# An attention and MLP kernel with a written-out order: the order and the PSUM banks are replaced, and the keep-busy products at the end are regrouped

## The chip, the cores and the metric

The kernel runs on one NeuronCore of a Trainium2 chip. A core has five instruction streams that run side by side: TensorE (PE, matrix products into PSUM), ScalarE (ACT), VectorE (DVE), GpSimd (POOL) and SyncE (SP), which here only issues transfers. Each runs its own list strictly in order, and the lists wait for each other through semaphores. PSUM has eight banks of 128 x 512 float32; TensorE writes a bank, ScalarE or VectorE reads it, and only then may TensorE write it again.

The metric is the device time of one execution in microseconds. Three runs of the kernel before took 799.29, 800.50 and 801.38 us (median 800.5).

## The reference

Sequence 2048, width 640, 32 heads of 20, everything in bfloat16.

```
x  = A_x                                  # (1, 2048, 640)
xn = layernorm(x)
qkv = xn @ wqkv                           # 640 x 1920; 32 heads of 20
p  = softmax(q @ k.T * 20**-0.5)          # 32 matrices of 2048 x 2048
s  = concat(p @ v) @ wo                   # attention branch
h  = gelu(layernorm(xn) @ w1)             # MLP branch
hs = concat(h, its four quarters shifted by +1, -1, +2, -2 rows) @ w2
x1 = xn + hs
b  = x1 + gelu(layernorm(x1) @ w3) @ w4
return x + s * silu(b)
```

Most of the work is the softmax: 32 x 2048 x 2048 exponentials.

## The kernel before

The program first writes itself down as a list of 6,035 tasks (`Planner.task`): each has an engine, what it reads and writes, a function that emits its one to 16 instructions, and, for a product, the kind of PSUM bank it takes (`acq`) and which task gives the bank back (`rel`). Costs and due times in the list (`dur`, `due`, `DUE`) play no part in what is emitted. The order is not computed: the string `TABLE` spells it out. `Planner.follow` (line 218) reads two characters for a task's number and one more for each bank choice, and appends the task to its engine's list. So the string fixes the order of each of the five engines and the bank of each product, and nothing else; `plan_sync` (line 322) then puts in the semaphore waits that the data and the banks require, and `emit` writes the instructions.

One thing in the instructions does depend on the order. A pair of score products (`score_pair`, line 1587 and 1600) can be written in two ways: as two products that use 32 of the 128 rows of TensorE's array each (called the row form here, line 1587), or as eight products that use 32 of its columns each and the zero-padded copies `QM` of the queries (the column form, line 1600). `follow` sets the row form where the task stands behind a row-form task or just ahead of one or of another score pair, else the column form:

```
if t.flex and (pe_mode or (nx is not None and (nx.mode or nx.flex))):
    t.mode, t.dur = 1, self.row_dur
```

The last block of queries is worked in two halves (`last_half`, line 1407 on), where the same choice is between lines 1458 (row form) and 1462 (column form), with 256 columns instead of 512.

The work is staged so. At the start x is loaded, normalised on VectorE, ScalarE and POOL, transposed through TensorE (line 1066, copied out at lines 1074 and 1077) and projected to keys and queries of the first four heads (`prep`) and to values (`v_proj`). The attention then goes through eight quads of four heads, and in each through four blocks of 512 queries (`attn_quad`). For each of 16 key tiles two score pairs are computed. Most pairs go to ScalarE's exponential (line 1647, 128 x 1024 at a time); the rest go to VectorE, which makes an approximate exponential by arithmetic on the bit patterns (line 1671 from PSUM, then lines 1565 on POOL and 1567 on VectorE). The products with the values (lines 1380 and 1579) add up in bank 7. `normalise` turns, scales and stores a block's result: on POOL (`onT`, line 1707), then by SP's transfers `on` (turned) and `o` (to memory).

In between run the projections of later heads (`stack`, five times), which go to memory and come back by SP's transfers `fKT`, `fQT` and `fa` (`fetch`); from these a transfer `qm` makes the copies `QM` of each block's queries, which its score pairs need. The MLP branch runs in the gaps of TensorE as well: `b_w1`, `b_w2`, `b_w3`, `b_w4`, nearly all of their products from line 719. Its Gelu runs on ScalarE in six long operations (`gelu1`, line 1962, and `gelu3`, line 2054), each behind the VectorE copies `gt` (line 2047) of all its inputs. In the last quad the output projection and the output's last steps are mixed in (`part_qc`, `finish_qc`: `woa`, `wob`, `cmb`, `st_out`).

At two places TensorE computes products that nobody reads, to stay busy: 41 at the start (`warm`, line 892), and near the end those of `keep_busy` (lines 1402 and 1407), whose number and form are listed in `FLN`: pairs of a form (1 is two products in the row form, 0 four in the column form) and a count.

## Time and profile before

| | |
|---|---|
| runs | 799.29, 800.50, 801.38 us |
| the profiled execution | 798.07 us, of which 796.3 us from first to last instruction |
| first exponential of the attention starts | 30.66 us |
| last exponential starts | 787.83 us |
| last product on TensorE starts | 791.35 us |
| granted TensorE clock, mean | 0.999 |

The table has times of one profiled execution; it was 2.4 us faster than the median of the three runs. Busy times in the profile are sums of instructions, and on one engine instructions overlap a little: an exponential is shown with 1041 ns although the next can start after 904 ns. So a busy share near 97% does not yet mean that an engine never waits. The column "idle before, releaser" of a group, and the view of waits, say how long an engine stood still ahead of such instructions and whose signal ended it.

By stretches of the span, as the windows view gives them, ScalarE was busy 41.80 us of the first 50, 97.36, 96.33, 98.31, 99.83, 99.01 and 99.97 us of the six hundreds from 100 to 700, 48.64 of 700 to 750 and 35.00 of the 46 us that are left.

### The profile page before, as it was taken

How to read it: one execution, taken by the hardware profiler on the slowest of the kernel's cores; microseconds unless marked ns; L12 is line 12 of the kernel's file. 1: busy time of each engine (PE TensorE's matmuls, PEld its weight loads, DVE VectorE, ACT ScalarE, POOL GpSimd, SP SyncE). 2: the span in 40 equal slices, each digit the busy share in tenths (PEclk: the TensorE clock that was granted, in tenths of full speed). 3: DMA queues.
4: the chain of work that ended last, by engine and by line, in shares of the span. 5: the costliest groups of instructions: out<-in, count | busy, mean ns of one | idle time of the engine just before them, and what ended most of it. 6: DMA issues, size and time to landing. Idle time of an engine off the chain costs nothing.

```text
span 796.3 us, 29914 instructions
## 1 busy us (share of the span) xinstructions
PE 776.1 (97%) x13408; PEld 323.0 (41%) x13408; DVE 733.0 (92%) x1206; ACT 766.3 (96%) x802; POOL 353.1 (44%) x208
## 2 busy tenths in 40 slices
PE   8999999999999999999999999999999999999996
PEld 4443333334444333333434444334333343445454
DVE  8879899989999999999999999999988989999967
ACT  7899999999999999999999999999999999999994
POOL 5535234251546737663532443544233243352453
PEclk9999999999999999999999999999999999999999
DMA  5022373342121323434233231325224113133432
GB/s 167 3 73 60 72 173 77 84 102 57 35 53 29 76 43 84 86 70 93 57 83 61 40 96 41 69 56 93 53 51 112 26 20 86 20 96 85 135 90 85
DMA packets 138671, 57.58 MB, mean 72 GB/s; under 512 B 111040, under 2 KB 133744, under 8 KB 138544
## 3 DMA queue, kind: packets, MB, share of 16 engines
q1 hardware_dynamic: 138544, 55.68, 30.4%
q8 instruction: 105, 1.72, 0.9%
q14 instruction: 22, 0.18, 0.1%
HBM read 34.70 MB, written 10.33 MB: 57 GB/s over the span
## 4 chain that ended last, share of the span: by engine, by line
PE 49%; ACT 35%; DVE 11%; DMA 2%; issue 1%; POOL 1%; SPq 0%; DVEq 0%; POOLq 0%
ACT arena L1647 30%; PE psum L719 18%; PE psum L1587 12%; PE psum L1579 8%; PE psum L1380 6%; DVE arena L1671 5%; PE psum L1600 5%; DMA out_dram<-arena 2%; DVE arena L1567 1%; ACT arena L2054 1%; ACT arena L1962 1%; ACT arena L1629 1%; DMA arena<-in_A_x_dram 1%; POOL arena L1870 1%; PE psum L1066 1%
## 5 line engine op out<-in xcount | busy, mean ns | idle before, releaser
L1647 ACT ACTIVATE arena<-psum 128x1024 bf16<-128x1024 f32 x726 | 676.4, 1041 | 15.7 <-PE psum L1587 8.9
L1671 DVE TENSOR_SCALAR arena<-psum 128x512 uint16<-128x512 f32 x536 | 342.0, 682 | 24.5 <-PE psum L1587 20.7
L1565 POOL TENSOR_TENSOR arena<-arena 128x2048 int32<-128x2048 int32 x68 | 244.5, 3598 | 252.6 <-DVE arena L1567 172.7
L719 PE MATMUL psum<-arena 128*32 128x320 bf16 (+1 forms) x5776 | 323.1, 332 | 2.3 <-DVE arena L1567 1.0
L1587 PE MATMUL psum<-arena 32*128 32x512 bf16 x1660 | 203.0, 384 | 8.0 <-ACT arena L1647 3.5
L719 PEld LDWEIGHTS psum<-arena 128*32 128x32 bf16 x5776 | 142.6, 96 | 116.5 <-issue 23.2
L1579 PE MATMUL psum<-arena 128*22 128x512 bf16 x2144 | 185.6, 381 | 0.0
L1567 DVE TENSOR_SCALAR arena<-arena 128x4096 uint16<-128x4096 uint16 (+1 forms) x151 | 164.2, 1105 | 2.0 <-PE psum L1579 0.8
L1380 PE MATMUL psum<-arena 128*22 128x512 bf16 x1448 | 138.7, 382 | 0.1
L1587 PEld LDWEIGHTS psum<-arena 32*128 32x128 bf16 x1660 | 56.7, 91 | 179.1 <-ACT arena L1647 96.9
L1600 PE MATMUL psum<-arena 128*32 128x512 bf16 x1296 | 98.5, 380 | 0.5 <-ACT arena L1647 0.2
L1579 PEld LDWEIGHTS psum<-arena 128*22 128x22 bf16 x2144 | 50.0, 91 | 64.4 <-issue 33.2
L1707 POOL TENSOR_TENSOR arena<-arena 128x512 bf16<-128x512 f32 x30 | 40.8, 1359 | 73.1 <-DVE arena L1567 40.2
L1380 PEld LDWEIGHTS psum<-arena 128*22 128x22 bf16 x1448 | 35.8, 90 | 50.8 <-issue 25.8
L1600 PEld LDWEIGHTS psum<-arena 128*32 128x32 bf16 x1296 | 27.1, 95 | 34.6 <-ACT arena L1647 28.0
L2047 DVE CAST arena<-psum 128x512 bf16<-128x512 f32 x48 | 32.9, 686 | 3.9 <-PE psum L719 3.2
L1256 DVE CAST arena<-psum 128x512 bf16<-128x512 f32 x40 | 26.7, 684 | 1.2 <-PE psum L719 0.7
L929 DVE BATCH_NORM_STATS2 arena<-arena 128x6 f32<-128x320 bf16 x54 | 24.3, 481 | 1.2 <-DMA arena<-in_A_x_dram 1.2
L1699 DVE STREAM_TRANSPOSE arena<-psum 128x512 f32<-128x512 f32 x31 | 22.0, 711 | 3.3 <-PE psum L1380 2.2
L1629 ACT ACTIVATE arena<-psum 128x2048 bf16<-128x2048 f32 x13 | 24.7, 1903 | 0.0
L1870 POOL TENSOR_TENSOR arena<-arena 128x640 bf16<-128x640 bf16 x12 | 16.7, 1397 | 15.6 <-DMA out_dram<-arena 6.2
L946 POOL TENSOR_SCALAR arena<-arena 128x640 bf16<-128x640 bf16 x16 | 14.0, 876 | 18.5 <-DVE arena L1567 9.4
(125 smaller groups left out, 364.8 us busy)
## 6 DMA issues: line engine op xcount, KB each, us to landing
arena<-in_B_w_dram SPq DMA_DIRECT2D x48, 160.0 KB, 2.7
arena<-arena SPq DMA_DIRECT2D x124, 32.0 KB, 1.9
arena<-in_B_w_dram SPq DMA_DIRECT2D x4, 960.0 KB, 5.6
arena<-in_A_x_dram SPq DMA_DIRECT2D x8, 320.0 KB, 5.7
arena<-in_A_x_dram SPq DMA_DIRECT2D x16, 160.0 KB, 2.3
out_dram<-arena SPq DMA_DIRECT2D x16, 160.0 KB, 2.4
heads<-arena SPq DMA_DIRECT2D x120, 20.0 KB, 2.1
arena<-queries SPq DMA_DIRECT2D x28, 80.0 KB
```

The costliest lines, as they stand in the source:

```text
L719: ins = e.matmul(pb[32 * c:32 * c + 32, 0:N], lhsT(k, c), rhs(k, c), start=(k == 0), stop=(stop and k == nk - 1), tile_position=(0, 32 * c))
L1380: ins = e.matmul(pb[32 * i:32 * i + 22, 0:512], VA[:, ql, kts[i // 2], i, :], PT[:, slots[i // 2][0].slot, 512 * (i % 2):512 * (i % 2) + 512],
L1565: return e.tensor_tensor(dst.bitcast(I32), U[:, ub, 0:w].bitcast(I32), bass.AP(c.tensor, c.offset, [list(c.ap[0]), [0, w // 2]]), op=ALU.add)
L1567: fa if onp else lambda e, v=v, dst=dst: e.tensor_scalar(dst, U[:, ub, 0:w], EXP_B[v], None, op0=ALU.add),
L1579: ins = e.matmul(pb[32 * i:32 * i + 22, 0:512], wv, dst[:, at:at + 512].bitcast(BF16), start=first, stop=final, tile_position=(0, 32 * i))
L1587: return e.matmul(out, self.KT[32 * i:32 * i + 32, b, 128 * kt:128 * kt + 128], self.QT[32 * i:32 * i + 32, b, 512 * qc:512 * qc + 512], s ...
L1600: ins = e.matmul(out[32 * c:32 * c + 32, :], self.KT[:, b, 128 * kt + 32 * c:128 * kt + 32 * c + 32], self.QM[:, gb, 2 * a + jj, :], start ...
L1629: lambda e: e.activation(self.PT[:, hp[0].slot:hp[0].slot + 2, :], self.psum[:, 512 * h0.slot:512 * h0.slot + 2048].rearrange("p (a b) -> ...
L1647: lambda e: e.activation(self.PT[:, hp.slot, :], self.psum[:, 512 * hs.slot:512 * hs.slot + 1024], AF.Exp, scale=cfg.scale),
L1671: lambda e, k=k, h=h: e.tensor_scalar(U[:, ub, 1024 * at + 512 * k:1024 * at + 512 * k + 512], self.bank(h.slot)[:, :], a_exp, EXP_BIAS, o ...
L1707: return e.tensor_tensor(OnT.rearrange("p (k d a) -> p a k d", k=4, a=4), Ob[:, :].rearrange("p (a k d) -> p a k d", a=4, k=4), in1, op=AL ...
L2047: T("dve", c_dve(512), lambda e, h=h, fc=fc, i=i, G=G: e.tensor_copy(G[:, i, fc, :], self.wbank(h)[:, 0:512]), reads=[wa], writes=at, name ...
```

## The change

Four things in the file change.

1. `TABLE` is replaced as a whole: 14,102 characters instead of 14,104. Every engine's order changes, and most bank choices do.
2. `FLN` is regrouped: 31 keep-busy tasks instead of 32 (12 instead of 13 in the row form, 19 in the column form as before).
3. `TP` is new: how many 128-column chunks of x a transposed bank holds. It is 1, and with 1 the rewritten loop makes the same tasks with the same instructions as before.
4. `OQ` is new: an addition to a transfer's latency in the task list. It is 0, and such latencies are not used for what is emitted.

```
+        self.OQ = 0.0
+        self.TP = 1
...
-        self.FLN = tuple( [(1, 2), (1, 1), (1, 2), (0, 4), (1, 2), (1, 2), (1, 3), (1, 1), (0, 4), (0, 11)])
+        self.FLN = tuple( [(1, 2), (0, 5), (1, 3), (0, 1), (1, 2), (1, 2), (1, 3), (0, 2), (0, 11)])
...
-            for kc in range(0 if g in cfg.TD else cfg.KC):
+            for kc in range(0, 0 if g in cfg.TD else cfg.KC, cfg.TP):
...
+                nk = min(cfg.TP, cfg.KC - kc)
+                for k in range(nk):
+                    for bi in range(4):
...
+                d = xnT[:, kc:kc + nk, 512 * g:512 * g + 512]
+                def fe(e, d=d, h=h, nk=nk, act=act):
+                    p = self.wbank(h, BF16)[:, 0:512 * nk].rearrange("p (k n) -> p k n", k=nk)
+                    return e.activation(d, p, AF.Copy) if act else e.tensor_copy(d, p)
...
-          name=f"otq{qc}", stream="otq", ndma=2)
+          dlat=cfg.OQ * (qc in cfg.SPL), name=f"otq{qc}", stream="otq", ndma=2)
...
 TABLE = (
-    r"#8#y$)&c###f#9#%#6#:#;$b#(#<#=#>#$#?#@#&#,$@#A#B#'#C#D#*#n#+#e&d$*$+#-#)#E$,#F$-#G#~#g#H#I$.#J#.#}#K$/#{$0%+)#d#L#M$2#N#z#O#P$3#k$K$##Q$1#|#R$$$%#s$4#"
...
```

Since a character pair is a task's number, the two strings can be read out into two lists of named tasks, and the lists compared. Names used below: `sc7_0_6_1` is a score pair (quad 7, block 0, key tile 6, second pair), `exp7_0_6_1` its exponential, `sh1_8a0` and `exph1_8_0` the same in the second half of the last block, `s6_2_2_3` a piece of the bit-pattern exponential of quad 6, block 2 (the last digit 3: on POOL, line 1565), `u` its first step on VectorE.

## The prediction

> **What bounds the kernel now.** I read the page first (busy shares, chain, costliest groups), then ScalarE's own waits in four stretches of the span, then single starts in the timeline.

> ```profile
> span 796.3 us, 29914 instructions
> PE 776.1 (97%) x13408; PEld 323.0 (41%) x13408; DVE 733.0 (92%) x1206; ACT 766.3 (96%) x802; POOL 353.1 (44%) x208
> ...
> PE 49%; ACT 35%; DVE 11%; DMA 2%; issue 1%; POOL 1%; SPq 0%; DVEq 0%; POOLq 0%
> ...
> L1647 ACT ACTIVATE arena<-psum 128x1024 bf16<-128x1024 f32 x726 | 676.4, 1041 | 15.7 <-PE psum L1587 8.9
> L1671 DVE TENSOR_SCALAR arena<-psum 128x512 uint16<-128x512 f32 x536 | 342.0, 682 | 24.5 <-PE psum L1587 20.7
> ```

> Three engines are nearly full, so no single one is the limit. Busy times overlap (an exponential lasts 1041 ns, but where ScalarE never waits the next starts 904 ns later), so I added up shortest distances from start to start. ScalarE's 726 exponentials then need 656 us, all its 785 operations about 738; VectorE's 1206 need 708; TensorE's work 731 (below). The span is 796: each has 7 to 11% in hand, and that is one engine waiting for another.

> ScalarE has least in hand. Its waits in 0 to 100, 100 to 400, 400 to 700 and 700 to 796 us (columns: total, times, longest):

> ```profile
> ACT arena L1647 <- PE psum L1587: 1.4, 1, 1.4
> ...
> ACT arena L1647 <- PE psum L1587: 6.2, 18, 0.6
> ACT arena L1647 <- PE psum L1380: 0.8, 3, 0.3
> ...
> ACT arena L1647 <- PE psum L1587: 0.9, 2, 0.5
> ...
> ACT arena L1647 <- PE psum L1458: 3.5, 4, 1.4
> ACT arena L1647 <- PE psum L1600: 1.1, 1, 1.1
> ```

> An order can win 7.0 us in 100 to 400 and about 5 at the end; in 400 to 700 there is nothing to win, and everywhere something to lose.

> **The change, part by part.** The new string holds the same tasks but for one keep-busy task. Read out against the task list, ScalarE's order hardly moves (629 of 785 in the old sequence, none more than 9 places off), VectorE's and TensorE's move by 2.8 and 4.6 places on average, and 456 of 2,034 bank choices stay.

> *TensorE's work.* The instructions are not quite the same. A score pair takes either form by its neighbours (lines 250 to 252): two products on row groups (L1587) or eight on column groups (L1600; L1458 and L1462 in the last block). The new order makes columns of 12 full and 7 half pairs more: 174 and 14 for 162 and 7. Start to start in the trace a column pair takes 432 ns (median of 56 before another product), a half one 433, a row pair 212, beside its partner in the same 212; a change of form costs 106 (a row pair before a product of L1579 takes 318). So 12 x 432 = +5.2; 7 x 433 = +3.0; 784 changes become 772, 12 x 106 = -1.3; the 19 row pairs and the keep-busy task that go save 3.2, or 159 each, since most ran beside a partner. Sum +3.8, to 734.7 us. Up to the exponential that began at 540 us the two lists of work agree (-0.04); +2.3 lies between there and 769, +1.5 behind.

> What hides it: TensorE's own pauses. From first to last product start are 789.5 us, 730.7 of them work; of the 58.8 of pauses 16.5 lie in 550 to 750, 5.9 behind. Without that cover all 3.8 is on the path, with it 0. In 550 to 750 I take 0, since ScalarE runs there in unbroken pieces. In the last block I take 0.7 of 1.5, about half: in the one place that I followed, the row pair `sh1_10a1` (784.62, its exponential at 785.04) gives way to the column pair `sh1_8a0` behind the same release, whose exponential can come only 0.25 later.

> *ScalarE's lead.* Of the exponentials after the first, 238 had no other TensorE task listed between their score pair and themselves; now 258. By the trace ScalarE loses (beyond 904 ns) a mean of 58 ns ahead of such a one, 45 with one task between, 58 with two, 24 with three, 32 with more; the counts go 80 to 90, 66 to 74, 79 to 67, 275 to 249. Weighted, +1.0 us. Bounds: 4.5 less (rival 2), or 20 times the mean wait of 100 to 400, 0.34, so 6.9 more. The value lies by the means because 236 cases stand behind the first.

> *Bank hand-overs.* TensorE tasks whose bank comes from ScalarE's latest listed operation fall from 322 to 277, from VectorE's latest from 255 to 245; more have one operation between. Each class by its mean pause (38 ns where only ScalarE's is tight, 45 only VectorE's, 85 both) gives +0.8 us of TensorE pauses: no relief. It goes into the same pauses: 0 in the sum, 0.8 in the bound.

> *SP's and POOL's queues.* Both run strictly in order, so a load stands behind whatever waits ahead of it. At the start `ld_wp_1` goes from 7th to 11th and `ld_wp_0` the other way; the 11th was issued at 8.45, such loads land within 8 us, and the first key product came at 19.6: hidden. Three copies of queries lose cover. (a) `qm7_0`, for the last quad's first score pair at 684.1, needs `fQT7`, now behind `on6_1` and `o6_1`; these need POOL's `onT6_1`, which moves behind `s6_2_2_3`:

> ```profile
> 655.48 1.35 POOL L1707 TENSOR_TENSOR arena<-arena 128x512 bf16<-128x512 f32 x1 [0.18 <-DMA heads<-arena]
> 661.29 3.60 POOL L1565 TENSOR_TENSOR arena<-arena 128x2048 int32<-128x2048 int32 x1 [4.47 <-PE psum L719]
> ```

> That piece ended at 664.9; with 1.4, 3.3, 3.4, 4.8 and 4.8 for the five steps behind it (durations of the same steps in the trace, landings estimated at 2 us after the issue) the copy lands at 682.6: 1.5 in hand where it was 10. (b) `qm1_1`, issued at 123.4, stands now behind `rr_2_0`, which needs VectorE's `hx_0_4` (136.2); with two shorter loads and its own 5.2 it lands near 143.8 for a pair at 144.7. (c) `qm6_0` goes behind `fKT6`, `fa6` and `o5_1`, with about 0 to 2 of the former 10. Covered they cost 0; uncovered ScalarE waits some 1 to 2 each, for exponentials are in order. I take 0.8 for the three, bounds 0 and 5.

> *The start.* `bn_stats` on rows 8 and 9 waited 0.25 us for its load, which now is issued earlier; against it `mx_0` stands before `norm12` and `norm13`, up to 0.9 late for transposes with 1.2 in hand. Net 0, between -0.3 and +0.9.

> *VectorE before the Gelu.* `gt_1_11` moves two places down; it ran at 389.50, its new place was 390.74, and it would end at 391.43, as ScalarE is ready for `gelu3_1` at 391.54. Cover 0.1; without it 0 to +1.2, taken as 0.

> *Keep-busy tasks.* 31 for 32, some moved by up to 3 us, all behind waits: 0. After 765 TensorE's pauses were at most 0.8 us.

> [...]

> Sum: 1.0 + 0.7 + 0.8 = +2.5 us. Span 798.8; the profiled run's 798.07 becomes 800.6. That run was 2.4 below the median of the runs shown, 800.5, so against the median **803.0 us**, +0.3%, just what a measurement here can tell from no change (0.3%, 2.4 us).

> **Rivals.**
> 1. *TensorE is the bound after all.* It leads the chain (49%). Then 3.8 and 0.8 land: +4.6, 805.1. Against: 58.8 us of pauses, and runs of 38.7 and 39.5 us of ScalarE alone in the chain.
> 2. *The loop closes earlier: faster.* Place: 100 to 400 us, where a bank freed by an exponential, the next score pair and the next exponential chase each other. The 45 tight hand-overs fewer save their mean 41 ns each and the 58 of the exponential behind: 45 x 99 = -4.5, 796.0. It decides if ScalarE's 7.0 us there fall below about 4. For it: 9 tight leads fewer in 140 to 193 us. Against: 8 more in 245 to 342.
> [...]
> 4. *The query copies come late*, two of them by 2 us: 807.0. For it: the cover lost at (a) to (c).

> That the change does nothing is no rival: most banks and places differ.

> **How the numbers follow.** Forecast 0.42 (own range 801 to 805.5), rival 1 0.14, rival 2 0.30, rival 3 0.03, rival 4 0.11. Half of the forecast lies within 798.1 to 802.9, half above; rival 2 is faster by over 0.3% in nine of ten. So faster 0.27, the same 0.24, slower 0.49. The range runs from 795.0 (rival 2 and a little of the end's 5 us) to 808.0 (rival 4).

> **What would show it.** L1600 x1392, L1458 x72, L1462 x224. ScalarE's waits on L1587 in 100 to 400: 6 to 8 us if I am right, below 4 for rival 2. A wait of 1 us or more at the first score pair of quads 6 or 7: rival 4. Waits of 2 to 4 in 400 to 700: rival 1. [...] Wrong I would be by one long wait that neither list shows.

## The result, and the profile after

Fifteen runs of the changed kernel took 797.15 us in the median (795.84 to 800.06), fifteen of the kernel before on the same chip 799.80 (798.32 to 802.55): a ratio of 0.9968, with a 95% interval of 0.9956 to 0.9981. On two other occasions, on two different chips, it was 0.9967 (0.9954 to 0.9981) and 0.9974 (0.9962 to 0.9985). So the change makes the kernel 0.3% faster, some 2.1 to 2.6 us, where +0.3% was forecast.

The page of the changed kernel, in the lines that answer to those shown of before (1647, 1587 and 1600 of before are 1650, 1590 and 1603 here, 719 is 721):

```profile
span 796.3 us, 30199 instructions
PE 777.7 (98%) x13562; PEld 323.3 (41%) x13562; DVE 729.8 (92%) x1206; ACT 766.9 (96%) x802; POOL 353.9 (44%) x208
...
PE 48%; ACT 43%; DVE 4%; DMA 3%; SPq 1%; issue 1%; POOL 0%; DVEq 0%
...
L1650 ACT ACTIVATE arena<-psum 128x1024 bf16<-128x1024 f32 x726 | 676.8, 1040 | 15.2 <-PE psum L1590 8.4
...
L1603 PE MATMUL psum<-arena 128*32 128x512 bf16 x1392 | 105.8, 380 | 0.3
```

The span is 796.3 us, to the tenth that of the profile of before, although the medians differ by 2.65. Neither profile is a typical execution: before was profiled at 798.07 us, below all fifteen of these runs, after at 798.06, above its median. One pair of profiles cannot show a difference of this size. So each experiment below also serves as one more trace of the parts of the old or the new order that it holds.

The view of ScalarE's waits, in 100 to 400 and in 700 to 797 us of the changed kernel:

```profile
ACT arena L1650 <- PE psum L1590: 5.7, 15, 0.6
ACT arena L1650 <- PE psum L1603: 1.1, 2, 0.7
ACT arena L1650 <- PE psum L1383: 0.8, 3, 0.3
...
ACT arena L1650 <- PE psum L1461: 3.2, 4, 1.1
ACT arena L1650 <- PE psum L1590: 0.3, 1, 0.3
```

In 100 to 400 they sum to 7.6 (7.0 before): nothing was won where rival 2 had put the gain. In 700 to 797 they fall from 5.0 (3.5, 1.1 and 0.4) to 3.5: the wait of 1.1 on a column pair is gone.

### Where the time goes, over all traces

In all traces the operations of ScalarE can be numbered, and the time of each set against the same number in the first trace of before. In most stretches two executions of one order agree within 0.02 us, so what differs can be placed. The table has the gain (-) or loss (+) of each stretch, against that first trace, over all traces that run the stretch in the old or the new order without an edit in it:

| stretch of the old order, us | old: traces, mean (range) | new: traces, mean (range) |
|---|---|---|
| 0 to 34.3 (start) | 8, -0.12 (-0.66 to 0.46) | 12, -0.51 (-0.92 to 0.27) |
| 34.3 to 126.1 | 8, 0.00 | 12, -0.51 (-0.51 to -0.50) |
| 126.1 to 137.7 | 8, 0.00 | 8, **+1.06** (0.75 to 1.72) |
| 137.7 to 335.2 | 7, -0.01 | 11, -0.71 (-0.77 to -0.55) |
| 335.2 to 601.2 | 8, +0.04 (-0.01 to 0.24) | 12, +0.62 (0.16 to 1.34) |
| 601.2 to 674.8 | 7, 0.00 | 11, +0.22 |
| 674.8 to 697.0 | 8, 0.00 | 9, **+0.33** (0.14 to 0.92) |
| 697.0 to 709.0 | 8, 0.00 | 12, +0.09 |
| 709.0 to 736.1 | 5, -0.42 (-1.12 to 0.00) | 12, **-1.85** (-1.90 to -1.32) |
| 736.1 to 784.2 | 3, -0.30 (-0.45 to 0.00) | 9, -0.12 (-0.18 to 0.23) |

The means add up to 0.6 us in favour of the new order by 784 us. The greatest single gain lies at 709 to 736 (1.4), the greatest losses at 126 to 138 (1.1) and at 675 to 697 (0.3).

Two rows hide something. In 335 to 601 about half of the new order's loss is a late load of weights at 470 us, for which the old order never waits. In the changed kernel it was issued at 463.40 and landed at 470.13:

```profile
470.17 1.00 PE L721 MATMUL psum<-arena 128*32 128x320 bf16 x24 [0.33 <-DMA arena<-in_B_w_dram]
```

Over the twelve traces this wait of TensorE is 0 to 0.48 us, and between 460 and 476 ScalarE loses 0.01 us where there is no wait and 0.61 where it is longest, 0.30 in the mean.

In the last row the old order scatters more than the table's three traces show. Between 768 and 776, seven traces of it that are unedited there lie at -0.45 to +1.30 (mean 0.00, the table's three -0.30), the new order's twelve at -0.68 to -0.28 (mean -0.64). In the slowest of the seven, old_fill, TensorE waits for POOL, and POOL for a load of x:

```profile
POOL arena L1870 <- DMA arena<-in_A_x_dram: 2.3, 1, 2.3
...
PE psum L719 <- POOL arena L1870: 0.8, 1, 0.8
```

With all seven the means would add up to 0.9 us in favour of the new order.

What comes behind 784 depends on the granted clock. In 5 of the 20 traces (new156_old, old637_new, old_sc, new_nobusy, new_rows; mean clock 0.995 to 0.997, in the others 0.998 to 1.000) it falls to half between 782 and 786, four times for one stretch of 3.41 us and once, in new_rows, for two. Behind 784.2 the other fifteen keep their distance from the first trace to 0.02 us; the four lose 1.18, 1.45, 1.48 and 1.57 us there, new_rows 1.97. The windows view of one of them (new156_old, below), then of the first trace of before. Columns: stretch, its length, busy time of PE, PEld, DVE, ACT and POOL with instructions, granted clock, DMA share, GB/s:

```profile
782.00:785.00 3.00, 2.85 (x38) 1.66 (x34) 2.48 (x3) 2.09 (x3) 2.67 (x2) 1.00 0.15 55
785.00:786.00 1.00, 0.99 (x20) 0.29 (x19) 0.76 (x3) 0.95 (x2) 0.00 (x0) 0.67 0.43 154
786.00:788.00 2.00, 2.00 (x37) 1.16 (x41) 1.93 (x5) 2.00 (x3) 0.00 (x0) 0.50 0.29 91
788.00:789.00 1.00, 1.00 (x28) 0.79 (x24) 0.11 (x1) 0.84 (x1) 0.00 (x0) 0.63 0.04 8
```

```profile
782.00:785.00 3.00, 2.85 (x41) 1.42 (x40) 2.24 (x3) 2.51 (x3) 1.96 (x2) 1.00 0.18 60
785.00:786.00 1.00, 0.77 (x27) 0.53 (x28) 0.97 (x4) 1.00 (x2) 0.00 (x0) 1.00 0.87 314
786.00:788.00 2.00, 2.00 (x72) 1.48 (x64) 1.97 (x4) 2.00 (x4) 0.00 (x0) 1.00 0.02 7
```

The reader is to see that TensorE was busy for 2.85 of 3.00 us ahead of the fall, just as where none came, and that 37 products began in the two slow microseconds where 72 did otherwise. One such fall lowers the mean clock of a run by 3.41 / 796 / 2 = 0.0021; half clock behind the last product, which costs nothing, lowers it by less than that (it takes the last 1.75 us of the span in the trace of before, from 794.51 on, and 2.98 in after). So, by this estimate, a run with a mean of 0.997 or less holds at least one real fall; of the 20 traces it is the five with a fall, and no other, that have such a mean. Of 118 runs of the kernel before (all those beside the experiments) 66 did, and took 799.70 us in the mean, against 798.71 for the 52 others; of 31 runs of the changed kernel 5 did (798.65 against 796.80; five runs make a rough mean). So the change made the falls rarer: 16% of the runs for 56%.

### The profile page after: what moved, and what is told of

It reads as the page before. It is cut to its first block, busy times and chain, and to the rows that moved or that the text cites. A ratio compares the mean times of both kernels' runs of the same rounds, so it can differ in the third digit from the quotient of the medians.

```text
span 796.3 us, 30199 instructions
## 1 busy us (share of the span) xinstructions
PE 777.7 (98%) x13562; PEld 323.3 (41%) x13562; DVE 729.8 (92%) x1206; ACT 766.9 (96%) x802; POOL 353.9 (44%) x208
## 4 chain that ended last, share of the span: by engine, by line
PE 48%; ACT 43%; DVE 4%; DMA 3%; SPq 1%; issue 1%; POOL 0%; DVEq 0%
ACT arena L1650 36%; PE psum L721 16%; PE psum L1590 11%; PE psum L1582 8%; PE psum L1383 6%; PE psum L1603 5%; ACT arena L2057 3%; DVE arena L1674 1%; ACT arena L1632 1%; ACT arena L1965 1%; DMA arena<-arena 1%; ACT arena L2085 1%; DMA arena<-in_B_w_dram 1%; PE psum L1465 1%; DVE arena L1570 1%; DMA arena<-in_A_x_dram 1%
## 5 line engine op out<-in xcount | busy, mean ns | idle before, releaser
L1590 PE MATMUL psum<-arena 32*128 32x512 bf16 x1636 | 197.5, 384 | 6.7 <-ACT arena L1650 3.7
L1582 PE MATMUL psum<-arena 128*22 128x512 bf16 x2144 | 181.5, 381 | 0.1
L1570 DVE TENSOR_SCALAR arena<-arena 128x4096 uint16<-128x4096 uint16 (+1 forms) x151 | 162.4, 1094 | 2.2 <-PE psum L1582 1.1
L1383 PE MATMUL psum<-arena 128*22 128x512 bf16 x1448 | 135.1, 382 | 1.7 <-DVE arena L1702 1.6
L1590 PEld LDWEIGHTS psum<-arena 32*128 32x128 bf16 x1636 | 54.7, 91 | 175.9 <-ACT arena L1650 93.5
L1603 PE MATMUL psum<-arena 128*32 128x512 bf16 x1392 | 105.8, 380 | 0.3
L1582 PEld LDWEIGHTS psum<-arena 128*22 128x22 bf16 x2144 | 49.2, 91 | 61.4 <-issue 28.4
L1383 PEld LDWEIGHTS psum<-arena 128*22 128x22 bf16 x1448 | 35.0, 90 | 53.1 <-issue 25.3
L1603 PEld LDWEIGHTS psum<-arena 128*32 128x32 bf16 x1392 | 29.2, 95 | 36.0 <-ACT arena L1650 26.3
L948 POOL TENSOR_SCALAR arena<-arena 128x640 bf16<-128x640 bf16 x16 | 13.9, 875 | 24.3 <-DVE arena L1570 15.7
L1809 DVE SCALAR_TENSOR_TENSOR arena<-psum,arena 128x320 bf16<-128x320 f32 x32 | 15.1, 487 | 8.3 <-PE psum L721 8.2
```

Source lines behind the costliest of these rows:

```text
L1383: ins = e.matmul(pb[32 * i:32 * i + 22, 0:512], VA[:, ql, kts[i // 2], i, :], PT[:, slots[i // 2][0].slot, 512 * (i % 2):512 * (i % 2) + 512],
L1570: fa if onp else lambda e, v=v, dst=dst: e.tensor_scalar(dst, U[:, ub, 0:w], EXP_B[v], None, op0=ALU.add),
L1582: ins = e.matmul(pb[32 * i:32 * i + 22, 0:512], wv, dst[:, at:at + 512].bitcast(BF16), start=first, stop=final, tile_position=(0, 32 * i))
L1590: return e.matmul(out, self.KT[32 * i:32 * i + 32, b, 128 * kt:128 * kt + 128], self.QT[32 * i:32 * i + 32, b, 512 * qc:512 * qc + 512], s ...
L1603: ins = e.matmul(out[32 * c:32 * c + 32, :], self.KT[:, b, 128 * kt + 32 * c:128 * kt + 32 * c + 32], self.QM[:, gb, 2 * a + jj, :], start ...
```

## The experiments

Each run was compared with the kernel before on the same chip. "Low" is the number of runs with a mean clock of 0.997 or less.

### Old and new order, spliced

A splice takes all tasks up to a point of one list, and then the others in the order and with the banks of the other list; at the points chosen no bank had to be changed.

```
TABLE = old[:exp1_1_5_0] + rest in new order     # old158_new
TABLE = new[:rz1_0]      + rest in old order     # new156_old
TABLE = old[:exp6_1_14_0] + rest in new order    # old637_new
TABLE = new[:exp6_1_8_0]  + rest in old order    # new637_old
```

> The old order and banks up to 158 us, the new ones behind. The new kernel measured 0.32% (2.6 us) faster. Theory M (rival 2 of the prediction: the loop of the middle closes earlier): the gain lies behind 158, so -2.6 us, ratio 0.997. Theory E (the ends carry it: the two profiles show the new order 0.6 us ahead at 126 us, 0.9 behind at 149, level at the end): the new part behind 158 brings -0.9, the old head adds nothing, so 0.997 to 0.999; then the half with the new head must be slower than before.

> The new order and banks up to 156 us, the old ones behind. Theory M: no change, ratio 1.000. Theory E: by the two profiles +0.9 us (ratio 1.001), with the loss at 130 to 134 us in the trace; if the typical run of the new kernel hasn't that loss, -0.7 (0.999).

> The old order up to 637 us, the new one behind. Theory M: no change, 1.000. Theory E: the end carries it: -1.0 us by the two profiles (0.9988), up to -2.6 if all of the gain lies at the end.

> The new order up to 637 us, the old one behind. Theory M: -2.6 us (0.997). Theory E: +1.1 by the two profiles (1.0013), 0 if the loss at 130 us is not typical.

Measured: 0.9996 (0.9987 to 1.0006), 1.0011 (1.0001 to 1.0021), 1.0009 (1.0000 to 1.0017), 1.0001 (0.9990 to 1.0012). None is as fast as the changed kernel, and the pairs don't add up to its gain. The reason is in the traces: at the splice each loses 1.9 to 2.5 us, since work that one order does early and the other late is left out of both. Their times decide nothing between the theories. Their traces help: away from the splice each repeats most stretches of one order to a few hundredths (the table), and two of them hold the fall of the clock.

The changed kernel again, for later comparison (0.9967, low 1 of 7; on the last chip 0.9974, low 1 of 9):

> The changed kernel once more, beside the three below. The hybrids of old and new order were no faster than before (0.9996 to 1.0011), so either the 0.32% repeats and the seams of the hybrids hid it, or it does not: 0.996 to 0.998 if it repeats, 1.000 if not. Theory G (the granted clock falls for one stretch of 3.41 us in the last block in most runs of before, 25 of 35 with a mean clock of 0.997 or less, and in few of the new kernel, 3 of 15): again 1 to 4 runs in 12 at 0.997 or less.

> The changed kernel again, on one chip with the next one. Ratio to before 0.9967 as twice before; 1 to 4 of 12 runs at a mean clock of 0.997 or less.

### The clock: what fills the array

Idle time doesn't tell the traces with a fall from those without. What comes nearest to it is how much of the array the products use. A row pair of the last block uses 32 rows, a quarter of the cells; four column products side by side use all (the eight of a column pair take 432 ns in the trace of before, twice the 216 between later warm-up products of as many columns). I weighted each product with rows times columns over 128 x 128 and with its length (0.417 ns for each column that streams through, half of what 427 ns for 512 columns make, the distance of the first warm-up products in the trace of before), and summed over successive stretches of 3.41 us, laid so that the clock's changes in the trace fall on their ends (the changes that the traces show lie multiples of 3.41 us from each other). Of 4,586 such stretches in the 20 traces five are followed by a fall; they were filled 0.297, 0.299, 0.303, 0.325 and 0.355. Of all others the emptiest was filled 0.324. Busy time does not set the five apart: TensorE was busy for 0.65 to 0.96 of their time, and the idlest of all stretches, busy 0.58 and filled 0.330, had no fall behind it. Nor does the number of products, 41 to 46 in the five and as few as 24 in others. In the old order all score and keep-busy products from 781.27 to 785.60 are row forms (only twelve products with the values, at 784.09, stand between them); in the new one a column pair (`sh1_8a0`) already comes at 784.37, and 781.35 to 784.37 is shorter than 3.41.

Three score pairs of the new order back to the row form, one of the old and of the new order to the column form:

```
-if t.flex and (pe_mode or ...):
+if t.flex and (t.name in ('sh1_8a0', 'sh1_8a1', 'sh1_10a1') or pe_mode or ...):    # new_rows
+if t.flex and t.name not in ('sh1_6a1',) and (pe_mode or ...):                     # old_col, new_col
```

> The new kernel with three half-width score pairs of the last block (sh1_8a0, sh1_8a1, sh1_10a1), which the new order writes in the column form, forced into the row form. Each stands alone between products of the other form, so it takes about the same time (212 plus two changes of 106, against 432 ns) but fills a quarter of the array's cells. Theory G: the filled share in the emptiest stretch of 3.41 us falls from 0.32 to 0.28, so more runs at a mean clock of 0.997 or less, some 4 to 8 of 12, and the median 0.3 to 1 us above the new kernel's. Theory O (the order's waits, not the clock, make the difference): shares as before, time within 0.3 us of the new kernel's or less.

> The kernel before with one half-width score pair of the last block (sh1_6a1) forced into the column form: it fills four times as many cells and breaks a stretch of 4.3 us in which TensorE runs the row form alone. Theory G: the emptiest stretch of 3.41 us rises from 0.29 to 0.35 filled, so nearly no run with a mean clock of 0.997 or less (0 to 2 of 12, against 25 of 35), and 0.7 to 1.0 us faster, ratio 0.9988. Theory O: the same share of low clocks, and 0.1 to 0.3 us slower, since the pair ends later.

> The new kernel with the same pair sh1_6a1 in the column form. Theory G: the emptiest stretch rises from 0.32 to 0.37, the few low runs (3 of 15) go, 0 to 1 of 12 left; the median 0 to 0.4 us below the new kernel's. Theory O: 0.1 to 0.3 us above it.

Measured: new_rows 0.9958 (0.9945 to 0.9972), low 1 of 6: no effect, against theory G's number, though so few runs say little about a share. The fall in its trace begins at 782.04, ahead of the first of the three pairs (782.50), so it is not their doing. old_col 0.9985 (0.9976 to 0.9995), low 0 of 10, as G had it; on the same chip 11 of 17 runs of the kernel before were low. new_col 0.9964 (0.9952 to 0.9977), low 0 of 5; its trace shows the price, 0.23 us by which the exponential behind the pair comes later.

The same without a touch on any score pair: three keep-busy tasks in the other form, and all of them left out (nothing that is read is left out):

```
-(1, 8)                       # FLN, forms by runs: eight in the row form
+(1, 4), (0, 5), (1, 1)       # old_fill: three of the eight become five column tasks
-FLN = ((1, 2), (0, 5), (1, 3), (0, 1), (1, 2), ...)
+FLN = ()                     # new_nobusy
```

> The kernel before with one group of its keep-busy products in the other form: three tasks in the row form (half the lines of two products that use a quarter of the array) become five in the column form (four products side by side that use all of it), in the same pause of 0.87 us ahead of sh1_6a1; no score pair changes its form. Theory G (the clock falls when the array was filled less than about a third over 3.41 us): the emptiest stretch rises from 0.29 to 0.35, so 0 to 2 of 12 runs with a mean clock of 0.997 or less (49 of 77 for the kernel before so far), and 0.5 to 0.8 us faster (ratio 0.9990 to 0.9994): two thirds of the 1.2 us by which such runs of the kernel before are longer. If the form of a product that nobody reads has no bearing: the old share, 1.000.

> The new kernel without its 31 keep-busy tasks. Theory G: by the traces 97 of 100 positions of the 3.41 us grid then have a stretch filled under a third, so nearly every run has a mean clock of 0.997 or less, most of them with two falls; 1.5 to 3 us slower than the new kernel, ratio to before 0.9985 to 1.001. If they only fill time: as the new kernel or up to 0.3 us faster, 0.9965 to 0.997.

Measured: old_fill low 1 of 11, ratio 0.9992 (0.9981 to 1.0004), the number that was expected, though its interval holds 1. new_nobusy low 10 of 11, ratio 0.9991 (0.9980 to 1.0002): without them the changed kernel loses most of its gain; this edit also adds idle time, so it does not tell the two apart. Over old_col, old_both and old_fill together 2 of 33 runs were low, against 66 of 118. That idle time is not the condition is shown by the traces (2.85 busy us of 3.00 ahead of a fall, and a stretch busy 0.58 without one behind it). That the filling is, is the author's theory, which they (0.297 to 0.355 ahead of the five falls) and the edits of the old order support; those edits also give TensorE a little more to run, and new_rows did not answer. No bound is shown, since one fall came at 0.355 and some stretches at 0.324 to 0.354 had none.

### 709 to 736: ScalarE's wait or TensorE's

In the old order a wait of ScalarE of 1.1 us ends at 720.38. The score pair that it waits for stands behind the output products `woa9_1`, and these wait at 718.36. The timeline of TensorE before:

```profile
716.95 0.40 PE L1579 MATMUL psum<-arena 128*22 128x512 bf16 x4
718.36 0.86 PE L719 MATMUL psum<-arena 128*32 128x320 bf16 x20 [1.01 <-DVE arena L1567]
```

The releaser named had been done for long; what came last was the transfer `otq2`: its second part was issued at 711.17 and landed 7.1 us later (the longest of its line). old_sc puts the score pair ahead of those products, old_both does that and has sh1_6a1 in the column form, old_qm moves a transfer:

```
-pvd7_1_0_3, woa9_1_0..2, woa8_0_0..4, woa8_1_0..1, sc7_1_11_1, woa8_1_2     # TensorE
+pvd7_1_0_3, sc7_1_11_1, woa9_1_0..2, woa8_0_0..4, woa8_1_0..1, woa8_1_2     # old_sc, old_both
-otq2, qm7_2, otq3                                                           # SP
+otq2, otq3, qm7_2                                                           # old_qm
```

> The kernel before with one score pair, sc7_1_11_1, put ahead of the products woa9_1 and woa8, which wait for the transfer otq2 (7.1 us from issue to landing in the trace). Theory T (the new order gains 1.9 us between 708 and 734 since no score pair stands behind that wait any more): ScalarE's wait of 1.05 us at 720 goes; it was 1.05, 0, 0.5 and 1.0 us in the four traces of the old order there, so 0.4 to 0.8 us faster, ratio 0.9990 to 0.9995. If the time comes back later in the block: 1.000.

> The kernel before with that pair moved and sh1_6a1 in the column form (which alone gave 0.9985). If the two causes add: 0.9975 to 0.998, some three fifths of the change's gain of 0.32%, with two edits; no runs at a mean clock of 0.997 or less. If T is wrong: 0.9985.

> The kernel before with one step of SP's queue moved: qm7_2 (four copies, needed at 733) goes behind otq3, so that the transfer otq2 shares its way with nothing. Theory P (at 716 to 734 TensorE is the bound of the old order: moving a score pair ahead of the wait gave ScalarE its 1.2 us at 720, and 1.3 were lost again by 734, since TensorE stood still all the same): otq2 lands in 5.5 us for 7.1, TensorE's wait of 1.0 us at 718 goes, and what is gained stays gained at 734: 0.4 to 1.0 us, ratio 0.9988 to 0.9995. If ScalarE's wait comes back later in the block all the same: 1.000.

Measured: old_sc 1.0004 (0.9995 to 1.0014), old_both 1.0010 (0.9997 to 1.0022), old_qm 1.0013 (1.0004 to 1.0023): none faster. ScalarE in old_sc, start and duration:

```profile
720.38 1.32 ACT L2082 ACTIVATE arena<-arena 128x1280 bf16<-128x1280 bf16 x1
722.47 2.85 ACT L1647 ACTIVATE arena<-psum 128x1024 bf16<-128x1024 f32 x3 [0.77 <-PE psum L1587]
...
726.66 1.94 ACT L1647 ACTIVATE arena<-psum 128x1024 bf16<-128x1024 f32 x2 [0.18 <-PE psum L1587]
728.75 2.85 ACT L1647 ACTIVATE arena<-psum 128x1024 bf16<-128x1024 f32 x3 [0.16 <-PE psum L1587]
```

The wait at 720 is gone (1.23 us won), and three others behind it give 1.33 back by 734. TensorE stands still no less than before: the pair, now ahead, waits for its bank, which an exponential has to give back first.

```profile
718.77 0.61 PE L1600 MATMUL psum<-arena 128*32 128x512 bf16 x8 [1.12 <-ACT arena L1647]
```

So the output products only come later, in front of the next pairs, and the edit has put one wait of TensorE in place of another. In old_qm the second part of `otq2` still takes 6.7 us, where 5.5 was expected; ScalarE's first wait is shorter by 0.4, and then VectorE waits 0.8 us for the load of x that now comes behind; 0.84 is lost by 734.

What TensorE's wait is worth, the table's five traces of the old order show without an edit in this stretch. Ahead of `woa9_1` TensorE stands still for 1.01, 0.94, 0.67, 0.16 and 0 us (before, old_col, old_fill, new637_old, new156_old), and the stretch takes 0, 0.07, 0.30, 0.63 and 1.12 us less than in the first trace. In the new order it is 1.9 less without such a wait, and 1.32 in old637_new, where TensorE waits 0.51. In the changed kernel TensorE has products with the values and score pairs to do until its output products begin, in new_again at 717.57, 6.0 us after `otq2` was issued and 0.4 after it landed, and shows no wait from 705 to 726. So the missing wait goes with some three fifths of what the new order is ahead of the first trace here. That this order of TensorE's work makes the 1.4 us, and nothing else in the stretch, was not tried by itself.

### What the new order loses, and a faster version

The loss at 126 to 138 is a chain of waits across five queues. The timeline of the changed kernel (SP's row: issue, then how long issuing took):

```profile
115.19 1.61 SPq L1719 DMA_TRANSPOSE arena<-arena  x1
122.72 3.97 SPq L1732 DMA_DIRECT2D heads<-arena  x4
...
128.13 1.34 POOL L1710 TENSOR_TENSOR arena<-arena 128x512 bf16<-128x512 f32 x1 [2.69 <-DMA heads<-arena]
...
130.35 0.40 PE L1383 MATMUL psum<-arena 128*22 128x512 bf16 x4 [1.20 <-DVE arena L1702]
```

The turning transfer `on0_1` goes out at 115.19 (104.45 before), behind ten copies and a large load; `o0_1` behind it waits for its landing; POOL's `onT0_2` waits for `o0_1`, VectorE's `ob0_3` for POOL, and the first product into bank 7 for VectorE. At the last quad's first score pair the copy `qm7_0`, issued at 680.23, is late:

```profile
685.00 0.39 PE L1582 MATMUL psum<-arena 128*22 128x512 bf16 x4
686.13 0.40 PE L1590 MATMUL psum<-arena 32*128 32x512 bf16 x4 [0.74 <-issue]
```

Both were mended in SP's order; new_all has sh1_6a1 in the column form besides, new_best instead five column keep-busy tasks for three in the row form:

```
-fa1, qm1_0, dk1_1, fKT1, ld_w2, on0_1, o0_1       # SP
+on0_1, fa1, qm1_0, dk1_1, fKT1, o0_1, ld_w2       # new_on, new_all, new_best
-on6_1, o6_1, fQT7, qm7_0
+on6_1, fQT7, o6_1, qm7_0                          # new_all, new_best
```

> The new kernel with one step of SP's queue put back: the turning transfer on0_1 stands again ahead of fa1 (the new order had it behind qm1_0, dk1_1, fKT1 and the large load ld_w2, issued at 114.6 us for 104.5), and ld_w2 behind o0_1. Theory S (that move costs the new kernel 0.75 to 1.7 us between 126 and 138 us in all six of its traces: TensorE waits 1.2 us for VectorE's ob0_3, this for POOL's onT0_2, this for the transfers o0_1): the wait goes, 0.8 to 1.3 us faster than the new kernel, ratio to before 0.9955. If the wait has another cause: as the new kernel, 0.997.

> The same, and fQT7 issued ahead of o6_1 (so qm7_0, for which TensorE waits 0.4 to 1.1 us at the last quad's first score pair, goes out some 5 us earlier), and the score pair sh1_6a1 in the column form. If all three causes are right: another 0.3 us (0.1 to 0.9 in the traces) and the few low clocks gone, so 1.3 to 2.0 us faster than the new kernel, ratio to before 0.9945 to 0.995; no wait of 0.3 us or more at the last quad's first score pair.

> The new kernel with on0_1 and fQT7 issued earlier and three keep-busy tasks in the row form replaced by five in the column form, in place of the score pair sh1_6a1 in the column form. Theory G and S: no low clocks, and the pair's exponential 0.2 us earlier than with the pair in the column form: as that kernel or 0.2 us faster, ratio to before 0.995. If the three parts don't add: 0.9965.

> The new kernel with on0_1 and fQT7 issued earlier and the three row-form keep-busy tasks as five in the column form, again. If its three parts are worth what the traces show (1.0, 0.3 and a fifth of 1.8 us), its mean lies 1.3 to 1.7 us below the new kernel's on this chip: ratio to before 0.9950. If 0.9953 was chance: 0.9967.

Measured: new_on 0.9967 (0.9954 to 0.9980): by its time no better than the changed kernel, which did not run beside it, though its trace loses 0.06 us at 126 to 138 where the changed kernel loses 0.75 to 1.72. new_all 0.9953 (0.9938 to 0.9968), new_best 0.9953 (0.9939 to 0.9967) and again 0.9955 (0.9940 to 0.9969), low 0 of 17 in the three; on the last chip its mean was 795.63 us, that of the changed kernel 796.87. In new_best the pair at the same place comes without a wait, the transfer `on0_1` at 101.29, and POOL without one at 124.80:

```profile
682.88 0.39 PE L1582 MATMUL psum<-arena 128*22 128x512 bf16 x4
683.21 0.40 PE L1590 MATMUL psum<-arena 32*128 32x512 bf16 x4
```

So new_best, at 0.9954, is faster than both kernels, than the changed one by 1.2 us where they ran side by side; what each of its three parts brings in time was not resolved, only in the traces (1.0, 0.2 and the rarer falls).

## Why the prediction was wrong, point by point

The time fell inside the range, on the other side of the starting point: -0.3% for +0.3%.

*TensorE's work.* The counts came as said (L1603 x1392, L1461 x72, L1465 x224), and what they add stayed hidden: busy time grew by 1.6 us, and 736 to 784 costs between 0.2 more (the table's three traces) and 0.1 less (all seven) than in the old order, where 0.7 had been taken. (730.7 and 3.8 make 734.5, not the 734.7 of the text; nothing hangs on it.) But a column pair was priced by its time alone. It also fills four times as many cells, and with more filling the falls of the clock were fewer (low 0 of 10 in old_col and 1 of 11 in old_fill, against 66 of 118). Together with the clock's share, worked out below, the term comes out at or below nothing.

*The last 90 us: the step that failed.* The prediction said that an order could win about 5 us of waits at the end, and then followed one place only, where a pair comes 0.25 later, and took +0.7 for the whole. For 550 to 750 it took 0, since ScalarE runs there in unbroken pieces; but the wait of 1.1 at 720, which stood among the lines that it showed, lies in there. What stands in front of it in either list, and that TensorE stood there for a transfer of 7.1 us, was not looked up. In place of the +0.7, this stretch alone gave -1.4 us.

*ScalarE's lead, +1.0.* The stretches 34 to 126, 138 to 675 and 697 to 709 sum to -0.3 in the new order, made of -0.5, -0.7 and +0.9, and 0.3 of the +0.9 is the late load at 470. Mean losses by how many tasks stand between pair and exponential say nothing about such sums.

*SP's and POOL's queues, +0.8.* The mechanism was right and its size too small: it cost 1.06 + 0.33 + 0.30 = 1.7. Of the three copies (a) came true: qm7_0 was late, and the stretch lost 0.14 to 0.92 us; its score pair began at 686.13 in the first trace, 0.09 behind the landing of the copy's last part, which had been worked out for 682.6. `on6_1` went out 1.3 us later than worked out (667.60), landed 4.5 us after its issue instead of 3.3, and the copy itself took 5.8 instead of 4.8. (b) and (c) cost nothing that the traces show. The largest loss, `on0_1`, and the load at 470 were not on the list: only copies that score pairs read were followed, not the transfers of results, whose buffer POOL needs back, and not the loads of weights.

*The start*, taken as 0, came out at -0.4, with a scatter of over a microsecond in either order. *gt_1_11*, 0: right, the traces show no step between 385 and 398.

*The clock.* The sum has no term for it. A fall in the last block, as something that the new order brings, was rival 3 of the chances, with 0.03; in truth it happens in 56% of the runs of the kernel before and in 16% of the changed one's. A pause need not go ahead of it: in new156_old the clock fell behind 2.85 busy microseconds of 3.00. In the traces full clock lasted 774.83, 778.24, 785.06, 788.48 or 791.89 us, which is 227, 228, 230, 231 and 232 times 3.413, and a fall lasted 3.41 us or, in new_rows, twice that. The profile at hand showed a run without one, and that this run was 2.4 us below the median was taken as a mere offset.

*The rivals.* Rival 2 named 796.0, close to what came, for a cause that is refuted: ScalarE's waits in 100 to 400 did not fall to its mark of 4, they are 7.6, and all that was won in the middle is 0.7 at 138 to 335. Rival 1 is refuted as a whole (more products, less time, 1.5 us of waits in 400 to 700 for its 2 to 4), though old_sc lets TensorE look like the bound from 716 to 734. Rival 4 came true in one copy, for 0.3 us.

How much of the gain is the clock? At the old share of low runs the changed kernel would lose 0.56 x 1.85 = 1.04 us to it, it loses 0.16 x 1.85 = 0.30; the old one 0.56 x 0.99 = 0.55. So 0.25 to 0.75 of about 2.2 us. By the 1.2 to 1.6 us that a single fall costs in the traces it is 0.40 x 1.4 = 0.6, and old_fill measured 0.6, with an interval that holds 0.

The rest is order. The traces place 0.6 to 0.9 of it, and since the runs without a low clock differ by 798.71 - 796.80 = 1.9, some 1.0 to 1.3 us of the typical run are not placed; their cause stays open. They are missing on the old order's side: its stretches add up to a run of 797.3 to 797.6 us (798.07 and the means), where its usual run without a fall takes 798.71. For the new order it is 796.7 against 796.80.

## What to carry to other kernels

Where a kernel's variants differ by a few tenths of a per cent, look at the spread of the runs and at the granted clock of each before the single profile is read: what the typical run loses may be absent from the one that was profiled. Price the form of a product not only by its time but by what the granted clock does behind it: here a run of score and keep-busy products all in the row form, from 781.27 to 785.60 us in the trace of before, went with low clocks in 66 of 118 runs, and where one column pair or five column tasks broke it, in 1 of 21 (old_col, old_fill). Whether this holds in another kernel was not tried. When an order written by hand is replaced, follow every transfer that has moved in a queue to whoever needs its buffer back, not only to whoever reads what it brings, and find out what stands in front of each long wait that the profile shows.
